# Converting double-precision weights in the first block: a narrower store for the low bits, clamps on GpSimd, casts on ScalarE

## The chip, the cores and the metric

The kernel runs on one core of one Trainium2 chip. The metric is the device time of one execution in microseconds (us); the kernel before takes 967.43 us (median of 3 runs, 966.49 to 967.93). Engines are named as in the profile: PE (TensorE matmuls), PEld (TensorE weight loads), DVE (VectorE), ACT (ScalarE), POOL (GpSimd) and SP (SyncE, which issues the transfers).

## The reference

Windowed attention over 2304 tokens (4 batches of 576, 8 heads of 64, window 64), then two feed-forward networks. The weight matrices arrive as float64, so each number is two 32-bit words; everything else is float32.

```python
h = x @ w_in                                   # 512 -> 2048
g = np.where(h > 0, h, np.exp(np.minimum(h, 0)) - 1)
x = g @ w_out                                  # 2048 -> 512
xn = x / np.sqrt(np.mean(x * x, -1) + 1e-6) * rms_g
gate, val = xn @ w_gate, xn @ w_val            # 512 -> 1536 each
out = (gate / (1 + np.exp(-gate)) * val) @ w_out2
```

## The kernel before

Tokens run through the first network in six blocks of 384. While PE works on a block, the attention of the next block is interleaved with it. A matmul here takes its operands as float32r pairs (a rounded high part and the remainder), three products for each: `mm_in` (line 381) is 12 matmuls of 384 columns for one of the 16 slices f of the hidden layer, `mm_y` (line 408) another 12. Block 1 runs from about 43 to 143 us.

In block 1 the weights of the first network are made as they are needed: the `Feeder` fw1 turns 32 tiles (w_in and w_out for f = 0 to 15) of 128x512 doubles into float32r pairs, which stay for blocks 2 to 6. A second `Feeder`, fwp, does the same for 36 tiles of the second network during blocks 2 to 5 and the start of the last stage; its tiles go on to a scratch tensor `pspill` or `ospill`. One tile takes these steps:

- a transfer brings the raw words (`big`, three buffers, or `tmp`); `lo` is the low word and `hi` the high word of each double
- `s1`: ACT takes the magnitude of `hi` (line 311) and scales the top bits of `lo` to a small integer of 0 to 7, stored as a 32-bit integer over `lo` (line 312); the magnitude is clamped (line 314), on DVE, in fw1 for every second tile on POOL; DVE shifts it left by 3 and ors in the low bits, reading two tensors (line 316)
- `sign` (line 323): DVE ors in the sign bit of `hi`; the raw tile is free after it
- `s2` (line 331): a cast to the high part of the pair, on DVE or ACT as the scheduler chooses
- `s3` (line 337): POOL subtracts to get the remainder

`step` does s3 of tile n-2, s2 of tile n-1 and s1 of tile n, so POOL's queue alternates subtractions and clamps. The tile `wm`, which holds a weight through these steps, has three buffers.

`x_split` (lines 364 and 365) makes the pair of a block's input, 4 casts and 4 subtractions on DVE. `elu` takes a matmul result through ACT (lines 399, 400) and DVE (line 401), and `split_g` makes its pair with a cast (line 390) and a subtraction (line 391) on DVE. A scheduler that simulates the program orders the instructions of every engine from this text; each engine then runs its queue in order. L202 to L224 are the softmax of the attention.

Of the kernel before, what the change touches and what calls it, by code (L numbers as in the profile page):

```python
# [9 lines left out]
F32R = mybir.dt.float32r  # L10
I32 = mybir.dt.int32
U32 = mybir.dt.uint32
AF = mybir.ActivationFunctionType
ALU = mybir.AluOpType
AX = mybir.AxisListType
# [5 lines left out]
def kernel(  # L21
# [17 lines left out]
    nc = tc.nc  # L39
# [9 lines left out]
    scale = 1.0 / float(D) ** 0.5  # L49
    BLOCKS1 = [384]*6  # L50
    MAX_M = (2.0 - 2.0 ** -20) * 2.0 ** 15 / 2.0 ** 112
# [232 lines left out]
    class Feeder:  # L284

        def __init__(self, src, raw, alloc, ahead, pool=False):
            self.pool = pool  # L290
            self.src, self.raw, self.alloc, self.ahead = src, raw, alloc, ahead
            self.n = self.loaded = 0
            self.r, self.m, self.u = {}, {}, {}

        def load(self, upto):
            while self.loaded < min(upto, len(self.src)):
                i = self.loaded
                r = self.raw()
                src = self.src[i][1]
                r = r.bitcast(I32)  # L300
                dst = r
                if len(src.shape) == 3:
                    dst = r.rearrange("p (k f) -> p k f", k=src.shape[1])
                nc.sync.dma_start(out=dst, in_=src)
                self.r[i] = r.rearrange("p (f t) -> p f t", t=2)
                self.loaded += 1

        def s1(self, i):
            lo, hi = self.r[i][:, :, 0], self.r[i][:, :, 1]
            m = mp.tile([128, 512], F32, tag="wm", name="wm", bufs=3)  # L310
            nc.scalar.activation(out=m, in_=hi.bitcast(F32), func=AF.Abs, scale=2.0 ** -112)
            nc.scalar.activation(out=lo, in_=lo.bitcast(U32), func=AF.Copy, scale=0.875 * 2.0 ** -29,
                bias=0.4999)
            (nc.gpsimd if self.pool and i % 2 else nc.vector).tensor_scalar(
                out=m, in0=m, scalar1=MAX_M, scalar2=None, op0=ALU.min)
            nc.vector.scalar_tensor_tensor(
                out=m.bitcast(I32), in0=m.bitcast(I32), scalar=3, in1=lo,
                op0=ALU.logical_shift_left, op1=ALU.bitwise_or)
            self.m[i] = m

        def sign(self, i):
            m, hi = self.m[i], self.r.pop(i)[:, :, 1]
            nc.vector.scalar_tensor_tensor(
                out=m.bitcast(I32), in0=hi, scalar=-2 ** 31, in1=m.bitcast(I32),
                op0=ALU.bitwise_and, op1=ALU.bitwise_or)
            return m

# [29 lines left out]
                self.step()  # L357


    def x_split(xt, n):  # L360
        r = []
        for kk in range(KD):
            xk = mp.tile([128, 2, NMAX], F32R, tag=f"x{kk}", name=f"x{kk}")
            nc.vector.tensor_copy(out=xk[:, 0, :n], in_=xt[:, kk, :n])
            nc.vector.tensor_tensor(
                out=xk[:, 1, :n], in0=xt[:, kk, :n], in1=xk[:, 0, :n].bitcast(F32),
                op=ALU.subtract)
            r.append(xk)
        return r
# [15 lines left out]
    def x_tile():  # L385
        return mp.tile([128, KD, NMAX], F32, tag="xt", name="xt")

    def split_g(src, n, copy):
        g = mp.tile([128, 2, NMAX], F32R, tag="g", name="g", bufs=1 + LAG)
        copy(out=g[:, 0, :n], in_=src[:, :n])  # L390
        nc.vector.tensor_tensor(  # L391
            out=g[:, 1, :n], in0=src[:, :n], in1=g[:, 0, :n].bitcast(F32), op=ALU.subtract)
        return g


    def elu(ph, n):

        e = mp.tile([128, NMAX], F32, tag="e", name="e", bufs=2)
        nc.scalar.activation(out=e[:, :n], in_=ph[:, :n], func=AF.Relu, scale=-1.0)  # L399
        nc.scalar.activation(out=e[:, :n], in_=e[:, :n], func=AF.Exp, scale=-1.0)  # L400
        nc.vector.scalar_tensor_tensor(  # L401
            out=e[:, :n], in0=e[:, :n], scalar=-1.0, in1=ph[:, :n], op0=ALU.add, op1=ALU.max)
        return split_g(e, n, nc.vector.tensor_copy)

    def mm_y(py, wt, g, n, first, last):
        for i, (a, c) in enumerate(((0, 0), (1, 0), (0, 1))):
# [347 lines left out]
    xt = x_tile()  # L754
# [7 lines left out]
        load_v(t)  # L762
    for s in range(NSTART):
        fw1.step()
    xs = x_split(xt, BLOCKS1[0])

    tok0 = 0
    pend = []
# [1 line left out]
    for b, n in enumerate(BLOCKS1):  # L770
        last = b == nblk - 1
        slots = {}
        if not last:
            nn = BLOCKS1[b + 1]
            xt = x_tile()
# [20 lines left out]
        gs = {}  # L796
# [5 lines left out]
        for f in range(F1):  # L802
            fw1.until(("in", f))
            ph = psum("w", 4)
            mm_in(ph, wu[("in", f)], xs, n, f == F1 - 1)
            gs[f] = elu(ph, n)
            run_slot(2 * f)
            if f == F1 - 1 and not last:
                xs_next = x_split(xt, nn)
            if b == 0:  # L810
                fw1.step()
            if f >= LAG:
                fw1.until(("out", f - LAG))
                mm_y(py, wu[("out", f - LAG)], gs.pop(f - LAG), n, f == LAG, False)
            run_slot(2 * f + 1)
            if b == 0:
                fw1.step()
# [7 lines left out]
        if not last:  # L825
            xs = xs_next
# [88 lines left out]
```

## Time and profile before

| what | value |
|---|---|
| median of 3 runs | 967.43 us (966.49 to 967.93) |
| the profiled execution | 967.15 us, its span 965.4 us |
| PE busy, share of the span | 918.5 us, 95% |
| DVE, ACT, POOL busy | 650.4, 491.9, 211.8 us |
| granted TensorE clock, mean | 0.986 of full speed |

The span is the time from the first to the last instruction in the trace; the execution is 1.75 us longer. Matmul ends are modelled, and consecutive matmuls overlap, so PE's busy share overstates how fast it advances: at full clock, 12 matmuls of 384 columns follow one another in 2.08 us. Idle time of an engine that is not the bottleneck costs nothing.

### The profile page before, as it was taken

How to read it: one execution, taken by the hardware profiler on the slowest of the kernel's cores; microseconds unless marked ns; L12 is line 12 of the kernel's file. 1: busy time of each engine (PE TensorE's matmuls, PEld its weight loads, DVE VectorE, ACT ScalarE, POOL GpSimd, SP SyncE). 2: the span in 40 equal slices, each digit the busy share in tenths (PEclk: the TensorE clock that was granted, in tenths of full speed). 3: DMA queues.
4: the chain of work that ended last, by engine and by line, in shares of the span. 5: the costliest groups of instructions: out<-in, count | busy, mean ns of one | idle time of the engine just before them, and what ended most of it. 6: DMA issues, size and time to landing. Idle time of an engine off the chain costs nothing.

```text
span 965.4 us, 16449 instructions
## 1 busy us (share of the span) xinstructions
PE 918.5 (95%) x5916; PEld 863.7 (89%) x5916; DVE 650.4 (67%) x1451; ACT 491.9 (51%) x1199; POOL 211.8 (22%) x228
## 2 busy tenths in 40 slices
PE   6678889999999999999999999999999999999998
PEld 5577789988889998899999999899998998998996
DVE  3899997858867786787788488178363276561461
ACT  5887755665666656566545456344141442341440
POOL 2465760146236114404402100200000000000000
PEclk9789989999999999999999999999999999999999
DMA  9556531765474265536438719781984737945621
GB/s 234 165 167 199 133 108 23 221 194 159 146 228 145 78 197 172 156 103 199 159 122 286 262 48 385 283 349 48 404 328 143 278 124 243 371 141 208 240 70 66
DMA packets 150402, 183.02 MB, mean 190 GB/s; under 512 B 81712, under 2 KB 111408, under 8 KB 150320
## 3 DMA queue, kind: packets, MB, share of 16 engines
q1 hardware_dynamic: 150320, 181.96, 57.3%
q8 instruction: 47, 0.77, 0.3%
q14 instruction: 35, 0.29, 0.1%
HBM read 144.18 MB, written 37.75 MB: 188 GB/s over the span
## 4 chain that ended last, share of the span: by engine, by line
PE 67%; DMA 6%; POOL 4%; ACT 4%; DVE 4%; issue 1%; SPq 0%; POOLq 0%; DVEq 0%; ACTq 0%
PE y L669 16%; PE w L669 12%; PE y L408 11%; PE w L381 10%; PE y L703 10%; PE w L703 5%; DMA pspill<-stg 5%; POOL stg L540 2%; ACT s L206 1%; ACT stg L539 1%; PE w L164 1%; POOL sw L569 1%; PE w L235 1%; PE w L222 1%; PE w L187 1%
## 5 line engine op out<-in xcount | busy, mean ns | idle before, releaser
L381 PE MATMUL w<-x,wu 128*128 128x384 f32 x1152 | 226.8, 345 | 15.3 <-DVE e L401 5.7
L408 PE MATMUL y<-g,wu 128*128 128x384 f32 x1152 | 223.7, 340 | 5.6 <-DVE g L390 3.0
L381 PEld LDWEIGHTS w<-x,wu 128*128 128x128 f32 x1152 | 203.8, 192 | 21.4 <-DVE e L401 6.1
L408 PEld LDWEIGHTS y<-g,wu 128*128 128x128 f32 x1152 | 198.6, 188 | 10.1 <-DVE g L390 4.2
L669 PE MATMUL y<-xw,pu 128*128 128x384 f32 x864 | 161.6, 334 | 0.0
L669 PEld LDWEIGHTS y<-xw,pu 128*128 128x128 f32 x864 | 151.2, 188 | 0.8
L540 POOL TENSOR_TENSOR stg<-wm,stg 128x256 fp32r<-128x256 f32 x72 | 62.5, 873 | 299.9 <-ACT stg L539 299.9
L669 PE MATMUL w<-xw,pu 128*128 128x384 f32 x648 | 123.7, 334 | 0.0
L635 DVE TENSOR_TENSOR c<-c,w 128x384 f32<-128x384 f32 x72 | 39.6, 550 | 118.1 <-PE w L669 117.3
L669 PEld LDWEIGHTS w<-xw,pu 128*128 128x128 f32 x648 | 113.3, 188 | 0.3
L703 PE MATMUL y<-wu,g 128*128 128x512 f32 x432 | 106.4, 390 | 0.0
L703 PEld LDWEIGHTS y<-wu,g 128*128 128x128 f32 x432 | 80.9, 188 | 16.2
L401 DVE SCALAR_TENSOR_TENSOR e<-e,w 128x384 f32<-128x384 f32 x96 | 52.6, 549 | 51.3 <-ACT e L400 50.1
L631 ACT COPY c<-y 128x384 f32<-128x384 f32 x72 | 34.5, 482 | 67.9 <-PE y L669 67.3
L391 DVE TENSOR_TENSOR g<-e,g 128x384 fp32r<-128x384 f32 x96 | 66.0, 689 | 1.8
L399 ACT ACTIVATE e<-w 128x384 f32<-128x384 f32 x96 | 46.3, 484 | 37.2 <-PE w L381 37.1
L337 POOL TENSOR_TENSOR wu<-wm,wu 128x512 fp32r<-128x512 f32 x32 | 47.3, 1489 | 42.7 <-ACT wu L331 27.6
L703 PE MATMUL w<-wu,g 128*128 128x512 f32 x216 | 55.9, 390 | 0.0
L651 ACT CAST g<-e 128x384 fp32r<-128x384 f32 x69 | 34.7, 511 | 37.5 <-DVE e L645 37.5
L206 ACT ACTIVATE s<-s,st 128x128 f32<-128x128 f32 x120 | 46.7, 392 | 10.9 <-DVE st L202 10.9
L640 ACT ACTIVATE e<-c 128x384 f32<-128x384 f32 x54 | 27.5, 524 | 47.1 <-DVE c L635 47.1
L400 ACT ACTIVATE e<-e 128x384 f32<-128x384 f32 x96 | 50.4, 526 | 1.7
(127 smaller groups left out, 1209.1 us busy)
## 6 DMA issues: line engine op xcount, KB each, us to landing
pu<-pspill SPq DMA_DIRECT2D x126, 512.0 KB, 6.5
pspill<-stg SPq DMA_DIRECT2D x84, 256.0 KB, 2.1
wu<-ospill SPq DMA_DIRECT2D x36, 512.0 KB, 5.2
big<-in_moe_w_out_dram SPq DMA_DIRECT2D x16, 512.0 KB, 5.3
big<-in_moe_w_in_dram SPq DMA_DIRECT2D x15, 512.0 KB, 3.8
vw<-in_v_dram SPq DMA_DIRECT2D x27, 256.0 KB, 3.6
tmp<-in_moe_w_out_dram SPq DMA_DIRECT2D x12, 512.0 KB, 4.7
big<-in_moe_w_gate_dram SPq DMA_DIRECT2D x12, 512.0 KB, 5.4
```

The lines of the kernel that those rows point to most:

```text
L206: nc.scalar.activation(out=s[:, p, :], in_=s[:, p, :], func=AF.Exp, scale=-1.0, bias=st[:, 0, p, :], accum_out=st[:, 1, p, :])
L337: eng.tensor_tensor(out=u[:, 1, :], in0=m, in1=u[:, 0, :].bitcast(F32), op=ALU.subtract)
L381: nc.tensor.matmul(pt[:, :n], lhsT=wt[:, a, kk * 128:(kk + 1) * 128], rhs=xs[kk][:, c, :n], start=(i == 0), stop=(i == len(seq) - 1))
L391: nc.vector.tensor_tensor(out=g[:, 1, :n], in0=src[:, :n], in1=g[:, 0, :n].bitcast(F32), op=ALU.subtract)
L399: nc.scalar.activation(out=e[:, :n], in_=ph[:, :n], func=AF.Relu, scale=-1.0)
L400: nc.scalar.activation(out=e[:, :n], in_=e[:, :n], func=AF.Exp, scale=-1.0)
L401: nc.vector.scalar_tensor_tensor(out=e[:, :n], in0=e[:, :n], scalar=-1.0, in1=ph[:, :n], op0=ALU.add, op1=ALU.max)
L408: nc.tensor.matmul(py[m][:, :n], lhsT=wt[:, a, m * 128:(m + 1) * 128], rhs=g[:, c, :n], start=(first and i == 0), stop=(last and i == 2))
L540: nc.gpsimd.tensor_tensor(out=t[:, 1, :], in0=src, in1=t[:, 0, :].bitcast(F32), op=ALU.subtract)
L635: nc.vector.tensor_tensor(out=t, in0=t, in1=bank[b, qi][:, :NB], op=ALU.add)
L669: nc.tensor.matmul(bank[key][:, :NB], lhsT=u[:, qi, a, kk * 128:(kk + 1) * 128], rhs=X[j][kk][:, x, :], start=(first and n == 0), stop=(n ...
L703: nc.tensor.matmul(po[m], lhsT=g[:, a, (m % 3) * 128:(m % 3 + 1) * 128], rhs=w[:, x, :], start=(first and i == 0), stop=(last and i == 2))
```

## The change

The low bits are no longer written over the low word: ACT's second operation stores them as 16-bit integers into the low half of the high word, whose low bits are not needed any more. So the shift on DVE reads one tensor, and `sign` masks the sign and the three low bits in one go (the mask grows by 7). The clamp gets a second operation, a maximum with 0.0, and in fw1 all 32 clamps go to POOL (fwp's stay on DVE). The casts of g in block 1 (16) and of x for blocks 1 and 2 (8) go from DVE to ACT.

```diff
                 self.r[i] = r.rearrange("p (f t) -> p f t", t=2)
+                self.low[i] = r.bitcast(U16).rearrange("p (f t) -> p f t", t=4)[:, :, 2]
...
-            nc.scalar.activation(out=lo, in_=lo.bitcast(U32), func=AF.Copy, scale=0.875 * 2.0 ** -29,
+            nc.scalar.activation(
+                out=self.low[i], in_=lo.bitcast(U32), func=AF.Copy, scale=0.875 * 2.0 ** -29,
                 bias=0.4999)
-            (nc.gpsimd if self.pool and i % 2 else nc.vector).tensor_scalar(
-                out=m, in0=m, scalar1=MAX_M, scalar2=None, op0=ALU.min)
-            nc.vector.scalar_tensor_tensor(
-                out=m.bitcast(I32), in0=m.bitcast(I32), scalar=3, in1=lo,
-                op0=ALU.logical_shift_left, op1=ALU.bitwise_or)
+            (nc.gpsimd if self.pool else nc.vector).tensor_scalar(
+                out=m, in0=m, scalar1=MAX_M, scalar2=0.0, op0=ALU.min, op1=ALU.max)
+            nc.vector.tensor_scalar(
+                out=m.bitcast(I32), in0=m.bitcast(I32), scalar1=3, scalar2=None,
+                op0=ALU.logical_shift_left)
...
-                out=m.bitcast(I32), in0=hi, scalar=-2 ** 31, in1=m.bitcast(I32),
+                out=m.bitcast(I32), in0=hi, scalar=-2 ** 31 + 7, in1=m.bitcast(I32),
...
-    def x_split(xt, n):
+    def x_split(xt, n, copy=nc.vector.tensor_copy):
...
-            nc.vector.tensor_copy(out=xk[:, 0, :n], in_=xt[:, kk, :n])
+            copy(out=xk[:, 0, :n], in_=xt[:, kk, :n])
...
-    def elu(ph, n):
+    def elu(ph, n, copy):
...
-        return split_g(e, n, nc.vector.tensor_copy)
+        return split_g(e, n, copy)
...
-    xs = x_split(xt, BLOCKS1[0])
+    xs = x_split(xt, BLOCKS1[0], nc.scalar.copy)
...
-            gs[f] = elu(ph, n)
+            gs[f] = elu(ph, n, nc.vector.tensor_copy if b else nc.scalar.copy)
...
-                xs_next = x_split(xt, nn)
+                xs_next = x_split(xt, nn, nc.vector.tensor_copy if b else nc.scalar.copy)
```

The scheduler moves instructions with it. POOL at the start of the weights, one clamp (L314 before, L318 now) or subtraction (L337, L342) per row; `wm` and `wu` carry the tile's number. Before:

```order
L314 TENSOR_SCALAR wm_445<-wm_445 128x512
L337 TENSOR_TENSOR wu_443<-wm_437,wu_443 128x512
L337 TENSOR_TENSOR wu_523<-wm_456,wu_523 128x512
L337 TENSOR_TENSOR wu_454<-wm_445,wu_454 128x512
L314 TENSOR_SCALAR wm_525<-wm_525 128x512
L314 TENSOR_SCALAR wm_595<-wm_595 128x512
```

and with the change:

```order
L318 TENSOR_SCALAR wm_437<-wm_437 128x512
L318 TENSOR_SCALAR wm_445<-wm_445 128x512
L318 TENSOR_SCALAR wm_456<-wm_456 128x512
L342 TENSOR_TENSOR wu_443<-wm_437,wu_443 128x512
L342 TENSOR_TENSOR wu_523<-wm_456,wu_523 128x512
L342 TENSOR_TENSOR wu_454<-wm_445,wu_454 128x512
L318 TENSOR_SCALAR wm_525<-wm_525 128x512
L318 TENSOR_SCALAR wm_536<-wm_536 128x512
L318 TENSOR_SCALAR wm_595<-wm_595 128x512
```

Every tile now has its clamp in POOL's queue, three of them ahead of the first subtraction, where one stood.

DVE where block 1 begins (x is the block's input pair, `big` and `tmp` are raw weights). Before:

```order
L314 TENSOR_SCALAR wm<-wm 128x512
L316 SCALAR_TENSOR_TENSOR wm<-wm,tmp_450 128x512
L323 SCALAR_TENSOR_TENSOR wm<-tmp_450,wm 128x512
L316 SCALAR_TENSOR_TENSOR wm<-wm,big_157 128x512
L323 SCALAR_TENSOR_TENSOR wm<-big_157,wm 128x512
L316 SCALAR_TENSOR_TENSOR wm<-wm,big_461 128x512
L364 CAST x_463<-xt 128x384
L364 CAST x_466<-xt 128x384
L364 CAST x_469<-xt 128x384
L364 CAST x_472<-xt 128x384
L323 SCALAR_TENSOR_TENSOR wm<-big_461,wm 128x512
L365 TENSOR_TENSOR x_463<-xt,x_463 128x384
```

and with the change:

```order
L320 TENSOR_SCALAR wm<-wm 128x512
L328 SCALAR_TENSOR_TENSOR wm<-big_157,wm 128x512
L320 TENSOR_SCALAR wm<-wm 128x512
L328 SCALAR_TENSOR_TENSOR wm<-tmp_450,wm 128x512
L370 TENSOR_TENSOR x_463<-xt,x_463 128x384
L370 TENSOR_TENSOR x_466<-xt,x_466 128x384
L320 TENSOR_SCALAR wm<-wm 128x512
L370 TENSOR_TENSOR x_469<-xt,x_469 128x384
```

The clamp and the casts of x are gone from DVE, and the shift (L320) reads `wm` alone. Between the start of block 1 and its end, DVE's queue has 10 casts of weights (L331, now L336) where it had 4; ACT has 6 fewer.

ACT at the first two hidden slices of block 1, with the change (`e` and `g` are a slice's activation and its pair):

```order
L404 ACTIVATE e<-w 128x384 x2
L315 ACTIVATE tmp_600<-tmp_600 128x512
L405 ACTIVATE e<-e 128x384 x2
L395 CAST g<-e 128x384
L314 ACTIVATE wm<-big_611 128x512
L336 CAST wu<-wm 128x512
```

The cast of g (L395) now stands in ACT's queue, between the activations and the next weight.

## Rows read from the trace of the kernel before

**Rows 1.** The page, its first line.

```profile
span 965.4 us, 16449 instructions
```

**Rows 2.** Busy PE, PEld, DVE, ACT, POOL by stretch; granted clock, DMA share, GB/s.

```profile
43.00:143.00 100.00, 85.06 (x600) 78.62 (x600) 97.05 (x188) 72.39 (x170) 64.09 (x42) 0.91 0.53 158
143.00:222.00 79.00, 76.80 (x603) 73.43 (x604) 59.75 (x156) 48.67 (x133) 21.39 (x26) 1.00 0.47 141
222.00:555.00 333.00, 324.44 (x2337) 311.13 (x2336) 254.90 (x605) 193.76 (x505) 103.35 (x122) 1.00 0.55 173
```

**Rows 3.** The waits of PE in 43 to 143 (total us, times, longest).

```profile
PE w L381 <- DVE e L401: 5.7, 2, 4.5
```

**Rows 4.** Groups of DVE in 43 to 143 by form: count | busy, mean | idle.

```profile
L323 DVE SCALAR_TENSOR_TENSOR wm<-big,wm 128x512 int32<-128x512 int32 x17 | 13.9, 824 | 0.1
L316 DVE SCALAR_TENSOR_TENSOR wm<-wm,big 128x512 int32<-128x512 int32 x16 | 13.3, 832 | 0.4 <-POOL wm L314 0.4
L390 DVE CAST g<-e 128x384 fp32r<-128x384 f32 x15 | 11.7, 779 | 0.4
L391 DVE TENSOR_TENSOR g<-e,g 128x384 fp32r<-128x384 f32 x14 | 10.8, 774 | 0.1
L314 DVE TENSOR_SCALAR wm<-wm 128x512 f32<-128x512 f32 x13 | 9.0, 690 | 0.0
L316 DVE SCALAR_TENSOR_TENSOR wm<-wm,tmp 128x512 int32<-128x512 int32 x10 | 8.9, 890 | 0.1
L323 DVE SCALAR_TENSOR_TENSOR wm<-tmp,wm 128x512 int32<-128x512 int32 x10 | 7.7, 772 | 0.0
L331 DVE CAST wu<-wm 128x512 fp32r<-128x512 f32 x4 | 3.2, 788 | 0.0
L364 DVE CAST x<-xt 128x384 fp32r<-128x384 f32 x3 | 3.1, 1072 | 0.0
```

**Rows 5.** POOL operations in 43 to 143, duration min/median/max in ns.

```profile
L314 POOL TENSOR_SCALAR wm<-wm x13: 1490/1782/2044, 48.4 to 136.7; 128x512 f32<-128x512 f32 x13
L337 POOL TENSOR_TENSOR wu<-wm,wu x29: 1277/1470/1860, 42.6 to 143.0; 128x512 fp32r<-128x512 f32 x29
```

**Rows 6.** DVE operations over the whole span, duration min/median/max in ns.

```profile
L316 DVE SCALAR_TENSOR_TENSOR wm<-wm,big x55: 675/686/1775, 22.1 to 606.2; 128x512 int32<-128x512 int32 x55
L323 DVE SCALAR_TENSOR_TENSOR wm<-big,wm x55: 652/691/1761, 22.8 to 606.9; 128x512 int32<-128x512 int32 x55
L390 DVE CAST g<-e x96: 344/360/1454, 57.3 to 548.5; 128x384 fp32r<-128x384 f32 x96
L391 DVE TENSOR_TENSOR g<-e,g x96: 542/558/1654, 60.0 to 548.9; 128x384 fp32r<-128x384 f32 x96
L314 DVE TENSOR_SCALAR wm<-wm x52: 395/426/1514, 15.9 to 605.7; 128x512 f32<-128x512 f32 x52
```

**Rows 7.** DVE beside POOL in order of time, 65 to 70 (start, duration).

```profile
65.33 3.38 POOL L337 TENSOR_TENSOR wu<-wm,wu 128x512 fp32r<-128x512 f32 x2
...
67.47 1.45 DVE L390 CAST g<-e 128x384 fp32r<-128x384 f32 x1
```

**Rows 8.** ACT: two groups of 43 to 143, and the page's g cast.

```profile
L331 ACT CAST wu<-wm 128x512 fp32r<-128x512 f32 x24 | 14.8, 617 | 14.7 <-DVE wm L323 14.7
L312 ACT ACTIVATE big<-big 128x512 int32<-128x512 uint32 x15 | 10.3, 684 | 5.9 <-DMA big<-in_moe_w_out_dram 3.0 <-DMA big<-in_moe_w_in_dram 2.8
...
L651 ACT CAST g<-e 128x384 fp32r<-128x384 f32 x69 | 34.7, 511 | 37.5 <-DVE e L645 37.5
```

**Rows 9.** DVE in order of time, 22.0 to 24.6, ahead of a softmax.

```profile
22.08 0.69 DVE L316 SCALAR_TENSOR_TENSOR wm<-wm,big 128x512 int32<-128x512 int32 x1 [1.38 <-ACT tmp L312]
24.54 0.28 DVE L202 CUSTOM_DVE_ANT_0 tmp<-w,mask 128x128 f32<-128x128 f32 x1
```

**Rows 10.** The chain that ended last in 43 to 143 (start, us).

```profile
125.00 3.59 DMA big<-in_moe_w_in_dram
```

**Rows 11.** A POOL operation on 256 columns, min/median/max in ns.

```profile
L569 POOL TENSOR_TENSOR sw<-sw,wm x12: 727/738/868, 191.1 to 462.5; 128x256 f32<-128x256 f32 x12
```

More of the change, by code (lines that the diff above doesn't have):

```diff
@@ L12 @@
 U32 = mybir.dt.uint32
+U16 = mybir.dt.uint16
 AF = mybir.ActivationFunctionType
@@ L292, in __init__ @@
             self.n = self.loaded = 0
-            self.r, self.m, self.u = {}, {}, {}
+            self.r, self.low, self.m, self.u = {}, {}, {}, {}
         def load(self, upto):
```

## The prediction

> **What bounds the kernel now.** I read the page first, then the table of busy time by stretch, then, for the one stretch that stands out, the waits of PE and the groups of DVE, POOL and ACT. The profiled execution takes 967.15 us, 0.28 below the median of the runs; its span is 965.4 [rows 1], and the sums below are made against it. By stretch [rows 2], PE is idle for 2.2 us of 79 in block 2 and for 8.6 of 333 in blocks 3 to 6, always at the full clock: PE sets the time there. Block 1, from 43 to 143 us, is different: PE is idle for 15 of 100 us and granted 0.91 of its clock, while DVE is busy for 97.05. PE's longest wait is for DVE (the activation at L401, 5.7 us) [rows 3]. So block 1 runs at DVE's pace. Block 2, which does the same matmuls and as much attention, takes some 80 us: about 20 us is the most that block 1 can give, and what it gives goes one for one to the end, since PE sets the pace of what follows.
>
> DVE is slow there partly because it waits inside its instructions. The cast of g takes 0.344 us at best but 0.779 on average in block 1 [rows 4, 6]; one that started during POOL's subtractions took 1.45 [rows 7]. Its wait is counted as busy time. Against the shortest duration of each [rows 6], the 26 shifts (13.3 + 8.9 us), 27 signs (13.9 + 7.7), 15 casts of g, 14 subtractions of g and 13 clamps of block 1 [rows 4] carry 4.7 + 4.0 + 6.5 + 3.2 + 3.9 = 22.3 us of waiting, beside 42 POOL operations: 0.53 us for each.
>
> **The change, part by part, in block 1.** DVE, from 97.05 us:
> - 13 clamps leave: -9.0 [rows 4].
> - 15 casts of g leave: -11.7; 3 casts of x (the fourth ran just before 43): -3.1 [rows 4].
> - 26 shifts read one tensor in place of two. No row shows a one-tensor shift. The nearest is the clamp, one input and one output of the same size, 0.690 on average [rows 4]: 26 x 0.690 = 17.9 in place of 22.2, so -4.3. The ends: nothing if it runs as it does now, and -11.9 if each reaches the clamp's best 0.395 [rows 6]. I take -4.3, because the same neighbour on POOL stays.
> - 6 casts of weights come from ACT by the scheduler's choice: 6 x 0.788 = +4.7 [rows 4].
> - 15 more POOL operations in the stretch (28 clamps in place of 13, the first 4 lying ahead of it): 15 x 0.53 = +8.0 of waiting.
>
> That leaves DVE at 81.7, say 82 us.
>
> POOL, now 64 us [rows 2], does 29 subtractions and 28 clamps. At the shortest durations [rows 5] that is 29 x 1.277 + 28 x 1.490 = 78.8 us, at the medians 29 x 1.470 + 28 x 1.782 = 92.5. Waiting for DVE makes the difference, and DVE gets some 15 us lighter, so I take the middle, 86. This prices the clamp with its second operation like the clamp with one. No row shows the dearer form; the ends are 0.727, the shortest POOL operation on half the columns [rows 11], and 2 x 1.490 = 2.98, a whole second pass. I take the one-operation price since it is the same tile on the same engine.
>
> ACT, 72.4 us [rows 2]: 15 casts of g and 3 of x at 0.511, less 6 casts of weights at 0.617 [rows 8]: +9.2 - 3.7 = 78 us. Its store of the low bits is priced as before, 0.684 [rows 8]: the same count of elements, every 8 bytes. If the narrow store took half as long again, 26 x 0.34 = 9 us would bring ACT to 87, level with POOL; if it were half as long, nothing would follow, since ACT would not be the bound.
>
> The longest queue becomes POOL with 86 us. DVE, which sets the pace now, is busy for 97% of the stretch; at that share block 1 takes 86 / 0.97 = 89 us, 11 less. Raw buffers work the same way: on the chain that ended last, a transfer of 3.59 us [rows 10] waits for a sign to free its buffer, and a clamp that takes 1.5 us on POOL in place of 0.4 on DVE lengthens that loop for half the tiles. I leave this inside the 3%.
>
> Ahead of block 1, DVE spends 22.08 to 24.54 on weights before it starts the softmax that ACT waits for [rows 9]. Of these four operations the clamp goes, a shift gets cheaper and one moves behind: 1 us, with 0 and 1.4 as ends.
>
> After block 1, 36 shifts of the second network's tiles get 0.26 us cheaper (medians 0.686 and 0.426 [rows 6]), and 4 casts of x for block 2 move. PE covers all this [rows 2]: 0. If PE's idle 10.8 us of blocks 2 to 6 shifted with the reordered queues, I allow 2 either way.
>
> **Sum:** 967.15 - 11 - 1 = 955.2; with the 0.28 us to the median, **955.5 us**. Without a row for the price of the new clamp, 950 to 961 is this case's own range (POOL from 81 to 91 us).
>
> The Trainium skill (SBUF — State Buffer, Who interferes with whom) speaks against the change: a GpSimd operation and a VectorE operation that reads two tensors from SBUF, or runs with two ports, exclude each other, and the later one fully blocks until the first is done. The trace agrees for single operations (1.45 us against 0.344), but on average 0.53 us of waiting falls to each POOL operation; if the rule held for each in full, the sum would be that of the third rival.
>
> **The rivals.**
>
> 1. *POOL has time to spare* (faster). Were the clamp with two operations as short as the lower end, 0.727, POOL would need 28 x 0.727 + 37.0 to 42.6 = 57 to 63 us and bind nothing; DVE with 82 would, and block 1 takes 82 / 0.97 = 84.5: 967.15 - 15.5 - 1 + 0.28 = 951. For it: the clamp with one input is slower on POOL than the subtraction with two, 1.490 against 1.277 [rows 5], so its time is not set by how much it reads. Against it: no row has it shorter. The Trainium skill (GPSIMD Engine Reference, section 3.1, Elementwise) says that up to two operations per element GpSimd is bound by its port, and gives 769 ns for 512 elements; by that price POOL's clamps would sum to 21.5 us and the time would be 951 too. The one-operation row here, 1.490 us, does not agree with it.
>
> 2. *The second operation costs a second pass on POOL* (slower). At 2.98 us a clamp POOL would need 28 x 2.98 + 37.0 = 120.4 us, block 1 124, and the kernel 967.4 + 24 - 1 = 990. It decides from the point where POOL's sum passes the 97 us that DVE has now: (97 - 42.6) / 28 = 1.94 us for a clamp at the median subtraction, 2.14 at the shortest. Between them and 2.98, say 2.3 us, it is 28 x 2.3 + 29 x 1.38 = 104, block 1 108, the kernel 974. For it: 1.94 is only 0.16 above the clamp's present median. Against it: the engine's queue is idle for 36 of 100 us now, and DVE gets lighter.
>
> 3. *The lock hands the gain back* (no change). If each of the 15 added POOL operations stops DVE for its whole 1.49 us and not for 0.53, DVE gets 22.4 in place of 8.0 and stands at 96, block 1 at 99: 967.4 - 1 - 1 = 965.5 to 967. For it: the single row of 1.45 us. Against it: the average over 42 operations.
>
> 4. *The change does not reach the end.* If block 1 shortens but its rest waits for transfers of raw weights, the gain is cut; the transfers fill 0.53 of their engines there [rows 2], which leaves room. I count this in the third.
>
> **How the numbers follow.** The forecast gets 0.38, the first rival 0.28, the third (with the fourth) 0.16, the second 0.18. A measurement of this kernel can tell 0.2%, some 2 us, from no change. Faster by over 0.2%: 0.38 + 0.28 + 0.06 of the third = 0.72; within it 0.10; slower 0.18. The range reaches from 946 (the first rival with a shift at its lower end and 2 us from the later blocks) to 968 (the third); only the second rival and a little at the lower end, some 0.2, lie outside.
>
> **What would show it.** The POOL clamp's duration decides first: 1.5 to 1.8 us is the forecast, 0.8 or less the first rival, over 1.9 the second. DVE busy in block 1 should fall to about 82 us in a stretch of some 89, POOL rise to 86, ACT to 78, PE's granted clock rise above 0.91, the casts of g on DVE be gone until block 2, and block 2 keep its length. DVE at 95 or more would speak for the third. The prediction is wrong if block 1 keeps its 100 us, or if blocks 2 to 6 change by over 3 us.

## The result, and the profile after

The changed kernel takes 975.65 us (median of 4 runs, 973.38 to 975.96) beside 967.68 us of the kernel before on the same chip (4 runs, 966.49 to 968.50): a ratio of 1.0078, 95% interval 1.0060 to 1.0097. It is 8 us slower. The forecast was 955.5 us, the range 946 to 968. The profiled execution took 975.55 us, its span is 973.8 us.

Line numbers after: abs L314, store of the low bits L315, clamp L318, shift L320, `sign` L328, cast L336, subtraction L342, casts of x L369, of g L395, `e` L404 to L406, `mm_in` L386, `mm_y` L413.

The same stretches as [rows 2], first PE, PEld, DVE, ACT, POOL, then granted clock, DMA share and GB/s:

```profile
43.00:143.00 100.00, 85.18 (x598) 77.70 (x597) 76.85 (x160) 91.82 (x182) 55.22 (x53) 0.93 0.51 148
143.00:222.00 79.00, 75.28 (x593) 71.54 (x592) 57.68 (x152) 52.20 (x133) 21.62 (x26) 1.00 0.47 141
222.00:555.00 333.00, 319.93 (x2298) 306.75 (x2297) 247.74 (x595) 208.00 (x503) 103.89 (x123) 0.99 0.53 166
```

DVE fell from 97 to 77 us, POOL from 64 to 55, and ACT rose from 72 to 92. PE did not get further in its 100 us. Its waits in 43 to 143 name another engine than [rows 3]:

```profile
PE y L413 <- ACT wu L336: 4.9, 4, 2.3
PE w L386 <- ACT wu L336: 4.3, 4, 1.6
```

The groups of ACT in the same stretch, as [rows 8], show why:

```profile
L315 ACT ACTIVATE big<-big 128x512 uint16<-128x512 uint32 x16 | 22.1, 1384 | 0.2
L315 ACT ACTIVATE tmp<-tmp 128x512 uint16<-128x512 uint32 x10 | 13.9, 1388 | 0.0
L336 ACT CAST wu<-wm 128x512 fp32r<-128x512 f32 x18 | 11.3, 626 | 1.7 <-DVE wm L328 1.6
L395 ACT CAST g<-e 128x384 fp32r<-128x384 f32 x15 | 8.2, 543 | 1.7 <-DVE e L406 1.6
```

The store as 16-bit numbers takes 1.38 us, where the store as 32-bit numbers took 0.684 [rows 8]; 26 of them are 36 us of ACT's 92. The casts of g and of weights cost about what they did before. DVE (groups as [rows 4]) and POOL (minimum, median, maximum in ns, as [rows 5]):

```profile
L320 DVE TENSOR_SCALAR wm<-wm 128x512 int32<-128x512 int32 x25 | 19.3, 774 | 4.5 <-POOL wm L318 4.5
L328 DVE SCALAR_TENSOR_TENSOR wm<-big,wm 128x512 int32<-128x512 int32 x16 | 14.3, 891 | 0.3
L406 DVE SCALAR_TENSOR_TENSOR e<-e,w 128x384 f32<-128x384 f32 x15 | 8.3, 552 | 13.5 <-ACT e L405 13.5
```

```profile
L318 POOL TENSOR_SCALAR wm<-wm x26: 604/628/1085, 44.4 to 137.5; 128x512 f32<-128x512 f32 x26
L342 POOL TENSOR_TENSOR wu<-wm,wu x27: 1271/1298/1734, 43.1 to 142.5; 128x512 fp32r<-128x512 f32 x27
```

The clamp with two operations takes 0.63 us on POOL; with one it took 1.78 [rows 5]. DVE now stands idle for 13.5 us until ACT has an activation ready.

**Where the 8 us lie.** 192 executions of each of the `mm_in` and `mm_y` lines make a block. Counted off in the traces, the last `mm_y` of each block is reached at these times (us from the span's start):

| block | 1 | 2 | 3 | 4 | 5 | 6 |
|---|---|---|---|---|---|---|
| before | 151.6 | 234.3 | 320.4 | 404.3 | 485.7 | 552.6 |
| after | 152.2 | 236.5 | 323.9 | 408.5 | 493.9 | 560.8 |

Block 1 ends 0.6 us later, blocks 2 to 5 together take 341.7 us in place of 334.1, and block 6 is unchanged. So two things want explaining: why block 1 gains nothing from 20 us less on DVE, and why blocks 2 to 5, whose loss I had forecast as zero, take 7.6 us more.

Blocks 2 to 5 before and after, in the columns of the first table:

```profile
151.60:485.70 334.10, 323.66 (x2491) 307.47 (x2490) 254.49 (x638) 206.37 (x560) 112.27 (x136) 1.00 0.52 159
```

```profile
152.20:493.90 341.70, 324.91 (x2484) 308.76 (x2483) 250.03 (x637) 221.29 (x558) 114.22 (x136) 0.99 0.51 155
```

ACT is busy for 14.9 us more; 26 stores at 0.70 us more each are 18. It is idle for a third of the time even so. But PE's idle time grew from 10.4 to 16.8 us. One such place in ACT's queue (start, duration, in brackets the idle time ahead):

```profile
282.49 0.41 ACT L544 CAST stg<-sw 128x256 fp32r<-128x256 f32 x1 [1.68 <-POOL sw L574]
282.80 0.58 ACT L225 COPY pT<-w 128x512 f32<-128x512 f32 x1
285.51 0.40 ACT L544 CAST stg<-wm 128x256 fp32r<-128x256 f32 x1 [2.13 <-DMA pspill<-stg]
285.82 0.48 ACT L404 ACTIVATE e<-w 128x384 f32<-128x384 f32 x1
286.20 0.58 ACT L172 COPY kT<-w 128x512 f32<-128x512 f32 x1
286.67 0.53 ACT L405 ACTIVATE e<-e 128x384 f32<-128x384 f32 x1
287.09 0.58 ACT L174 COPY qT<-w 128x512 f32<-128x512 f32 x1
```

and PE beside it:

```profile
284.13 1.15 PE L236 MATMUL w<-pT,vw 128*64 128x64 f32 x32
287.73 3.12 PE L386 MATMUL w<-x,wu 128*128 128x384 f32 x12 [2.45 <-ACT qT L174]
```

A cast into a staging buffer of the second network (`stg`, two buffers) stands 2.13 us until the transfer to the scratch tensor frees its buffer. Behind it in the same queue are the activation of h and the two copies out of PSUM that PE needs. PE stops for 2.45 us, and its next 12 matmuls then take 3.12 us, where a row of twelve elsewhere shows 2.24:

```profile
319.89 2.24 PE L386 MATMUL w<-x,wu 128*128 128x384 f32 x12
```

The granted clock of 288.2 to 296.2 is 0.79, so a part of it ran at the lower of the two levels (1.2 and 2.4 GHz), after 1.00 in the 8 us before. Here one wait is paid twice. That isn't the rule: two pauses of 2.34 and 2.44 us in the same blocks were followed by 8 us at a granted clock of 1.00, and at this place the kernel before has a pause too, of 1.46 us. The three waits for the copies in the attention (`kT` before, `qT` after) grew by 3.0 us, not by the whole loss:

```profile
PE w L381 <- ACT kT L177: 4.2, 3, 1.6
```

```profile
PE w L386 <- ACT qT L174: 7.2, 3, 2.4
```

Another 3.8 us lie in shorter waits of PE for DVE (2.0 us before, 5.8 after); how the stores lengthen those was not traced.

### The profile page after: what moved, and what is told of

Read it like the earlier page. It is cut to its first block, busy times and chain, and to the rows that moved or that the text cites. A ratio compares the mean times of both kernels' runs of the same rounds, so it can differ in the third digit from the quotient of the medians.

```text
span 973.8 us, 16471 instructions
## 1 busy us (share of the span) xinstructions
PE 922.7 (95%) x5916; PEld 866.4 (89%) x5916; DVE 621.4 (64%) x1418; ACT 538.1 (55%) x1216; POOL 203.5 (21%) x244
## 4 chain that ended last, share of the span: by engine, by line
PE 67%; ACT 15%; DMA 7%; POOL 4%; issue 3%; DVE 3%; SPq 0%; POOLq 0%; ACTq 0%; DVEq 0%
PE y L674 15%; PE w L674 12%; PE w L386 11%; PE y L413 10%; PE y L708 10%; PE w L708 5%; DMA pspill<-stg 4%; ACT wm L314 3%; POOL stg L545 2%; ACT big L315 2%; ACT tmp L315 2%; ACT s L207 2%; ACT e L404 1%; ACT e L405 1%; DMA big<-in_moe_w_gate_dram 1%
## 5 line engine op out<-in xcount | busy, mean ns | idle before, releaser
L386 PE MATMUL w<-x,wu 128*128 128x384 f32 x1152 | 228.3, 346 | 19.2 <-ACT qT L174 7.2
L413 PE MATMUL y<-g,wu 128*128 128x384 f32 x1152 | 225.6, 342 | 10.2 <-ACT wu L336 4.9
L386 PEld LDWEIGHTS w<-x,wu 128*128 128x128 f32 x1152 | 204.2, 192 | 25.6 <-ACT qT L174 7.6
L413 PEld LDWEIGHTS y<-g,wu 128*128 128x128 f32 x1152 | 199.5, 189 | 16.6 <-ACT wu L336 5.9
L406 DVE SCALAR_TENSOR_TENSOR e<-e,w 128x384 f32<-128x384 f32 x96 | 52.9, 551 | 75.1 <-ACT e L405 74.0
L315 ACT ACTIVATE big<-big 128x512 uint16<-128x512 uint32 x55 | 75.9, 1381 | 0.7
L404 ACT ACTIVATE e<-w 128x384 f32<-128x384 f32 x96 | 47.5, 496 | 40.9 <-PE w L386 36.5
L544 ACT CAST stg<-wm 128x256 fp32r<-128x256 f32 x72 | 29.1, 409 | 46.2 <-DMA pspill<-stg 31.9
L342 POOL TENSOR_TENSOR wu<-wm,wu 128x512 fp32r<-128x512 f32 x32 | 44.3, 1387 | 46.0 <-ACT wu L336 27.6
```

The lines of the kernel that those rows point to most:

```text
L315: nc.scalar.activation(out=self.low[i], in_=lo.bitcast(U32), func=AF.Copy, scale=0.875 * 2.0 ** -29, bias=0.4999)
L342: eng.tensor_tensor(out=u[:, 1, :], in0=m, in1=u[:, 0, :].bitcast(F32), op=ALU.subtract)
L386: nc.tensor.matmul(pt[:, :n], lhsT=wt[:, a, kk * 128:(kk + 1) * 128], rhs=xs[kk][:, c, :n], start=(i == 0), stop=(i == len(seq) - 1))
L406: nc.vector.scalar_tensor_tensor(out=e[:, :n], in0=e[:, :n], scalar=-1.0, in1=ph[:, :n], op0=ALU.add, op1=ALU.max)
L413: nc.tensor.matmul(py[m][:, :n], lhsT=wt[:, a, m * 128:(m + 1) * 128], rhs=g[:, c, :n], start=(first and i == 0), stop=(last and i == 2))
```

## The experiments

The theories that the expectations name: **A**, the 16-bit store fills ACT, and ACT sets block 1's pace; **A2**, the loss sits in blocks 2 to 5, through the second network's stores; **B**, the casts on ACT are too much; **C**, the clamps on POOL hold DVE up; **D**, the three `wm` buffers set block 1's pace; **E**, it is the order of the queues and the hops between engines. A *miss* is a measurement outside the range that a theory had named. Times in the text are medians; block times come from the one profiled execution of each, and since single runs of one kernel often lie 2 to 3 us from its median, smaller differences of a block are not read.

### Each part alone, and the change without one

**e1_wide**: the change with the 32-bit store, the shift that reads two tensors and the old mask (not in the cut below), so that POOL's clamps and ACT's casts are what remains.

```diff
-                out=self.low[i], in_=lo.bitcast(U32), func=AF.Copy, scale=0.875 * 2.0 ** -29,
+                out=lo, in_=lo.bitcast(U32), func=AF.Copy, scale=0.875 * 2.0 ** -29,
...
-            nc.vector.tensor_scalar(
-                out=m.bitcast(I32), in0=m.bitcast(I32), scalar1=3, scalar2=None,
-                op0=ALU.logical_shift_left)
+            nc.vector.scalar_tensor_tensor(
+                out=m.bitcast(I32), in0=m.bitcast(I32), scalar=3, in1=lo,
+                op0=ALU.logical_shift_left, op1=ALU.bitwise_or)
```

> The low bits are stored again as 32-bit integers over the low word and the shift reads two tensors; clamps with two operations on POOL and casts on ACT stay. Theory A (the 16-bit store, 1.38 us in place of 0.68, makes ACT the queue that sets block 1 and delays the later blocks): ACT in block 1 falls from 92 to some 76 us, block 1 from 100 to 85 or 90 us, blocks 2 to 6 return to their old length, 952 to 960 us in all. Theory B (the casts moved to ACT are what is too much for it): 970 us or more. Theory C (32 clamps on POOL hold DVE's ports and give back what they save): no better than 966.

Measured: 974.28 us (970.75 to 977.94, 6 runs), ratio 1.0076 (1.0055 to 1.0096). Block 1 ends at 158.8, 7.2 us later than before; blocks 2 to 5 take 334.0 us, as before. Its block 1:

```profile
43.00:143.00 100.00, 83.54 (x557) 74.57 (x556) 77.80 (x147) 75.50 (x177) 55.60 (x50) 0.90 0.51 150
```

No engine but PE is busy for over 78% of it, and still block 1 is longer than before. For block 1 theory A misses: with ACT relieved, something holds it that is no engine's sum. For blocks 2 to 5 it is right. B and C had this time in their ranges; the next runs take the two parts one by one.

**e2_narrow_only**: before with the 16-bit store, the one-tensor shift and the wider mask; clamps and casts as before.

> The kernel before with the 16-bit store alone (and with it the one-tensor shift and the wider sign mask). Theory A: the store takes 1.38 us in all 68 tiles; block 1 stays near 100 us because DVE and ACT are both near 92, and blocks 3 to 5 get longer by 4 to 8 us in sum, 970 to 978 us. Theory B: ACT without the casts has room, 965 to 968. Theory C says nothing of it.

Measured: 977.73 us (975.60 to 979.30, 5 runs), ratio 1.0107 (1.0090 to 1.0124). Block 1 ends at 149.9, and blocks 2 to 5 take 346.1 us, 12 more than before. This part alone costs all that the change costs, and costs it outside block 1, as A had it (blocks 3 to 5 take 7.9 us more, of its 4 to 8).

**e3_clamps_only**: before with the two-operation clamps, all of the first network's on POOL.

> The kernel before with the clamps alone: two operations, all 32 of the first network on POOL. Theory A: the clamp takes 0.63 us on POOL in place of 1.49, DVE loses 9 us of clamps and much of its waiting; block 1 falls to 85 to 92 us, 954 to 961 us in all. Theory C: DVE's waiting grows by what the clamps saved, 966 or more. Theory B says nothing of it.

Measured: 969.75 us (967.25 to 974.77, 12 runs), ratio 1.0018 (1.0005 to 1.0032). The profiled execution is the slowest of the twelve, so its block 1 (157.0) says little. DVE is busy for 85 of 100 us and POOL for 59; nothing is gained, so A misses and the time is in C's range. C's mechanism is there in part: in this execution the shifts and signs of block 1 sum to 25.9 and 24.9 us, 7 us more than before [rows 4], against the 9.0 us of clamps that left. But DVE's sum fell all the same.

**e4_casts_only**: before with the casts of g and x on ACT, as in the change.

> The kernel before with the casts alone: g in block 1 and x for blocks 1 and 2 on ACT. Theory A: DVE loses 15 us in block 1, ACT rises from 72 to about 80, block 1 falls to 88 to 93 us, 956 to 962 us in all. Theory B: ACT holds up the activations, 969 us or more.

Measured: 968.00 us (965.84 to 969.27, 12 runs), ratio 1.0006 (0.9996 to 1.0015). Block 1 ends at 151.3. Both ranges miss, and B falls: by themselves the casts cost nothing, and give nothing.

**e5_narrow_fw1**: the change, but with the 16-bit store and the one-tensor shift in the first network only; the second network's 36 tiles as before.

```diff
+            if self.pool:
                 nc.scalar.activation(
                     out=self.low[i], in_=lo.bitcast(U32), func=AF.Copy, scale=0.875 * 2.0 ** -29,
                     bias=0.4999)
+            else:
+                nc.scalar.activation(out=lo, in_=lo.bitcast(U32), func=AF.Copy, scale=0.875 * 2.0 ** -29,
+                    bias=0.4999)
```

> The changed kernel with the 16-bit store and the one-tensor shift in the first network's tiles alone; the second network's 36 tiles get the 32-bit store and the shift that reads two tensors. Theory A2 (the 8 us are lost in blocks 2 to 5, where ACT's store is 0.7 us longer in each of the second network's tiles and PE waits for ACT's copies behind it): block 1 as in the changed kernel, blocks 2 to 5 as before, 966 to 969 us. Rival: the loss comes from block 1's reordered start into block 2, then 973 us or more remain.

Measured: 967.72 us (965.13 to 969.66, 12 runs), ratio 1.0000 (0.9989 to 1.0011). Block 1 ends at 151.6 and blocks 2 to 5 take 334.6 us. A2 holds: the 16-bit store in the second network's tiles costs the whole 8 us, and block 1 of the change is worth nothing either way.

### The prices by themselves

**p1_prices**: before, with the operations in question run three times each behind the last output, on data that is there.

> The kernel before, and behind its last output, when the engines are idle, three times each: ACT's store of the low bits as 32-bit at 8 bytes, 16-bit at 8 bytes, 16-bit at 4 bytes, 16-bit packed, 32-bit packed and bfloat16 at 8 bytes; POOL's clamp with one and with two operations; DVE's one-tensor shift. If the 16-bit store is dear because it writes half of a word, the packed one takes 0.68 us and the one at 4 bytes 1.38; if it is the integer type, packed takes 1.38 too and bfloat16 0.68. POOL's clamp: 1.49 us with one operation, 0.60 with two. The shift: 0.42 us.

ACT first, 512 numbers of 32 bits read at every 8 bytes (minimum, median, maximum in ns): L896 writes 32-bit numbers every 8 bytes, L899 16-bit every 8, L902 16-bit every 4, L905 16-bit side by side, L907 32-bit side by side, L909 bf16 every 8. Then POOL's clamp with one operation (L913) and with two (L916).

```profile
L896 ACT ACTIVATE probe<-slot x3: 673/704/719, 963.0 to 972.1; 128x512 int32<-128x512 uint32 x3
L899 ACT ACTIVATE probe<-slot x3: 1313/1317/1336, 963.6 to 972.7; 128x512 uint16<-128x512 uint32 x3
L902 ACT ACTIVATE probe<-slot x3: 820/826/827, 964.7 to 973.7; 128x512 uint16<-128x512 uint32 x3
L905 ACT ACTIVATE probe<-slot x3: 628/631/632, 965.4 to 974.4; 128x512 uint16<-128x512 uint32 x3
L907 ACT ACTIVATE probe<-slot x3: 643/648/648, 965.9 to 974.9; 128x512 int32<-128x512 uint32 x3
L909 ACT ACTIVATE probe<-slot x3: 1320/1325/1327, 966.5 to 975.5; 128x512 bf16<-128x512 uint32 x3
L913 POOL TENSOR_SCALAR probe<-slot x3: 1480/1485/1651, 961.7 to 966.1; 128x512 f32<-128x512 f32 x3
L916 POOL TENSOR_SCALAR probe<-slot x3: 608/609/777, 963.2 to 967.6; 128x512 f32<-128x512 f32 x3
```

Neither the type nor the stride is dear alone: 16-bit numbers side by side take 0.63 us, 32-bit numbers every 8 bytes 0.70. Two bytes written at every eighth take 1.32. And the clamp with one operation takes more than twice as long as the one with two, here with hardly a neighbour (three shifts on DVE ran in the same 6 us). Of the expectations, two missed: at every 4 bytes the store takes 0.83 and not 1.38, and the shift, beside POOL's clamps, took 0.57 and twice 0.82 us and not 0.42. The run takes 979.42 us, the probes included.

The Trainium skill (ScalarE: Activation LUTs, section What ACT_TABLE_LOAD costs) gives one element per cycle for every function, with constant scale and bias 186 ns and 0.833 ns for each column: 613 ns for 512, an estimate from that page. The rows for outputs side by side (0.63 and 0.65) agree; the strided 16-bit output is not covered by it.

### Block 1 and the buffers of `wm`

A tile takes a `wm` buffer at abs and gives it back after the subtraction. Averaged over tiles 7 to 31 of the first network, from the start of abs to the end of the subtraction, and from there to the abs that takes the buffer next (operations paired in the order in which they ran):

| kernel | buffers | held, us | free, us | (held + free) / buffers | a tile every | block 1 ends |
|---|---|---|---|---|---|---|
| before | 3 | 9.79 | 1.37 | 3.72 | 3.70 | 151.6 |
| after | 3 | 9.40 | 1.86 | 3.75 | 3.78 | 152.2 |
| e1_wide | 3 | 10.03 | 2.18 | 4.07 | 4.04 | 158.8 |
| s8_wide_2wm | 2 | 7.52 | 1.09 | 4.31 | 4.34 | 168.7 |
| s7_wide_4wm_1stg | 4 | 11.13 | 3.84 | 3.75 | 3.85 | 151.0 |
| s1_wide_5wm | 5 | 12.35 | 5.67 | 3.60 | 3.66 | 147.6 |

The two rates agree because a buffer goes round as tiles go through, so their agreement proves nothing. With two or three buffers one is taken again 1 to 2 us after it came free, and with four and five it lies there for 4 to 6. The lower three rows are the experiments that follow.

**e7_wide_buf** and **e8_before_buf**: `wm` of the first 20 tiles from the pool of the finished weights, so that no tile waits for one of three buffers; on e1_wide and on before.

```diff
-            m = mp.tile([128, 512], F32, tag="wm", name="wm", bufs=3)
+            if self.pool and i < 20:
+                m = wp.tile([128, 1024], F32, tag="wu", name="wm")[:, 0:512]
+            else:
+                m = mp.tile([128, 512], F32, tag="wm", name="wm", bufs=3)
```

> 32-bit store, clamps on POOL, casts on ACT (the first experiment of this list) and for the first 20 tiles a weight buffer of its own in place of one of three. Theory D (block 1 goes at the pace of three weight buffers: a tile holds one for about 10 us and 2 more pass until it is taken again, so one tile per 4 us, whatever engine is free): the first 20 tiles run at 2.5 to 3 us each, block 1 loses 10 to 20 us, 953 to 964 us. Rival E (queue order and hops between engines set the pace, not the buffers): 971 us or more.

> The kernel before with the same extra weight buffers. Theory D: DVE is busy for 97 of 100 us, so buffers give little here, 0 to 4 us: 963 to 968 us. If buffers alone set the pace in every version it gains as much as the wide version does, 955 us or less. Rival E: no change, 966 to 969 us.

Measured: 1007.10 us (1005.85 to 1007.96, 4 runs) and 998.26 us (997.94 to 1001.32, 4 runs). D misses in both, and E in the second. The scheduler laid these tiles out almost one after the other: the first abs comes at 32 us and not at 15, a tile follows every 4.5 and 4.1 us, and block 1 ended at 193.0 and 180.3. So they are no test of D. But with more buffers than e1_wide and before, block 1 ends 34 and 29 us later, so the order of the queues can do much by itself, which is E's point.

**s1_wide_5wm**: e1_wide with five buffers, which `wm` and the staging tiles share (the same memory as three and two).

```diff
-            m = mp.tile([128, 512], F32, tag="wm", name="wm", bufs=3)
+            m = mp.tile([128, 512], F32, tag="wm", name="wm", bufs=5)
...
-        t = mp.tile([128, 2, 256], F32R, tag="stg", name="stg", bufs=2)
+        t = mp.tile([128, 2, 256], F32R, tag="wm", name="stg", bufs=5)
```

> 32-bit store, clamps on POOL, casts on ACT, and the weight tile's three buffers and the two of the staging tile (which is idle in block 1) made one set of five. Theory D (in block 1 a tile holds one of three buffers for 10 us, so one tile passes per 3.4 to 4 us although no engine is full): with five, block 1 falls from 110 us to 85 to 92, then DVE or PE sets it; 948 to 960 us. Rival E (the order of the queues and the hops between engines set the pace): block 1 stays over 105 us, 968 us or more.

Measured: 963.92 us (961.60 to 965.20, 6 runs), ratio 0.9954 (0.9938 to 0.9971): faster than both kernels. Block 1 ends 11.2 us earlier than in e1_wide (D had 18 to 25), blocks 2 to 5 take 332.6 us. The time lies between the ranges of D and E, and the profiled execution is the fastest of the six. The same stretch:

```profile
43.00:143.00 100.00, 88.09 (x630) 83.68 (x627) 90.06 (x162) 82.18 (x194) 59.68 (x52) 0.93 0.52 153
```

All engines do more in the same 100 us, and DVE is once more the fullest.

**s7_wide_4wm_1stg**: e1_wide with four `wm` buffers and one for staging, not shared. **s8_wide_2wm**: e1_wide with two `wm` buffers.

> The change with the 32-bit store and the two-tensor shift, as in e1_wide, but four wm buffers and one stg buffer, each with its own tag: nothing is shared in block 1. Theory D (the three wm buffers set the pace of block 1 once no engine is full): block 1 ends at 147 to 152 us in place of e1_wide's 158.8, as with the five shared buffers (147.6). Rival (s1_wide_5wm gained through the sharing of wm and stg, or through another order): block 1 ends within 2 us of 158.8. With one stg buffer blocks 2 to 5 should get longer, since every staging cast then waits for the transfer of the one before it: total 968 to 985 by D, 980 or more by the rival.

> e1_wide with two wm buffers in place of three, the opposite test. In e1_wide a tile holds its buffer for 10.03 us and the next one takes it 2.18 us later, three buffers, so 4.04 us per tile. Theory D: with two buffers it is (10.0 + 2.2) / 2 = 6.1 us per tile if the steps take as long, at least 5.0 if the shorter queues cut the buffer's cycle to 10 us; 32 tiles then make block 1 longer by 30 to 65 us and the time 1000 to 1040 us. Rival (queue order and not buffers): within 10 us of e1_wide's 974.

Measured: s7 995.58 us (989.36 to 996.68, 4 runs), s8 996.24 us (one run). Block 1 of s7 ends at 151.0, as D had it; its total is above what D expected, because with one staging buffer blocks 2 to 5 take 339.6 us, block 6 takes 77.0 in place of 66.8, and all that follows 426.7 in place of 412.8, a larger loss than I had priced. In s8 block 1 ends at 168.7: 10 us later than in e1_wide, where D had 30 to 65, since a tile comes every 4.34 us and not every 5 or more (a buffer is held for 7.52 us and not 10); blocks 2 to 5, which use `wm` too, take 346.1. The 996.24 us are just below D's 1000 and well above the rival's range. PE's longest waits in block 1 of s8 are for the steps of the weights:

```profile
PE w L385 <- ACT wu L335: 12.1, 9, 2.7
PE w L385 <- POOL wu L341: 5.1, 7, 1.4
```

With 2, 3, 4 and 5 buffers and no other edit that touches block 1, it ends at 168.7, 158.8, 151.0 and 147.6. So the number of buffers moves block 1. It doesn't do so in e1_wide by making an engine wait for one, as D has it. Abs on ACT takes the buffer, and a subtraction on POOL frees it. From 15 to 165 us ACT stands idle ahead of abs in e1_wide for a transfer alone, and in s8 for that subtraction, 4.7 us in 5 places (1.5 us before, 0.3 in the change):

```profile
L314 ACT ACTIVATE wm<-big x19: 647/663/721, 19.2 to 146.2; 128x512 f32<-128x512 f32 x19
L314 ACT ACTIVATE wm<-tmp x13: 644/665/722, 15.4 to 117.3; 128x512 f32<-128x512 f32 x13
  DMA big<-in_moe_w_in_dram: 1.8, 1
```

```profile
  POOL wu L341: 4.7, 5
```

No abs of e1_wide starts less than 0.3 us after its buffer came free. What is left is that the scheduler, which simulates the program with these buffers, orders the queues by them, and the engines then run that order: closer to E than to D. No run kept the order and altered the buffers, so this is not shown, and why e1_wide's order is 7 us worse than that of before or of the change stays open. Transfers of raw weights, the prediction's fourth rival, made ACT wait in block 1 for 9.5 us before and 2.6 in the change: they are not what keeps the change from gaining.

### Five shared buffers in the other versions

**s6_after_5wm** is the change itself, **s4_fw1_5wm** e5_narrow_fw1, **s2_before_5wm** before, **s3_clamps_5wm** e3_clamps_only and **s5_casts_5wm** e4_casts_only, each with the edit of s1_wide_5wm.

> The changed kernel whole, with five buffers. Theory A2: blocks 2 to 5 keep most of the 8 us that the 16-bit store costs there; 966 to 975 us, and 6 to 9 us above the version with the narrow store in the first network alone. Rival: more staging buffers free ACT from its waits there, and the two versions are within 3 us.

> The change with the 16-bit store in the first network's tiles alone, and five buffers. Theory A for block 1 (ACT, 92 of 100 us busy with stores of 1.38 us, sets its pace): block 1 loses 3 to 7 us at most, 960 to 966 us. If ACT's load is not what sets it and buffers are, it falls as far as the wide version, 950 to 958 us.

> The kernel before with the same set of five buffers. Theory D with DVE as the bound beside it: DVE is busy for 97 of 100 us, so block 1 loses at most 4 us, 962 to 967 us. If the buffers alone set the pace before the change too: 950 to 958 us.

> Before with the two-operation clamps, all on POOL in the first network (as e3_clamps_only), and five buffers for wm and stg together. Theory D with DVE as the next limit: e3_clamps_only had DVE busy for 85 of 100 us and block 1 to 157.0 us; with five buffers block 1 ends at 147 to 151 and the time is 962 to 966 us, so that the casts on ACT are not needed for the gain. Rival (DVE must be lightened by the casts too, as s2_before_5wm, which starts block 1 4 us late and ends it at 164): 970 to 980 us.

> Before with the casts of g and x of the first block on ACT (as e4_casts_only) and five buffers for wm and stg together. If DVE sets the pace (92 of 100 us in e4_casts_only), five buffers change block 1 by under 2 us from 151.3, or start it some 4 us later as in s2_before_5wm: 966 to 972 us. If the buffers set it (a tile's cycle of 7.92 + 2.88 us over three buffers gave 3.76 us per tile), block 1 ends at 144 to 149 and the time is 960 to 966 us.

| run | time, us | ratio to before | block 1 ends | blocks 2 to 5 |
|---|---|---|---|---|
| s6_after_5wm | 968.40 (966.51 to 971.72, 12) | 1.0005 (0.9993 to 1.0017) | 152.3 | 333.3 |
| s4_fw1_5wm | 970.14 (966.72 to 973.57, 12) | 1.0020 (1.0007 to 1.0033) | 153.0 | 335.7 |
| s2_before_5wm | 981.13 (977.00 to 983.18, 6) | 1.0128 (1.0106 to 1.0150) | 164.3 | 335.8 |
| s3_clamps_5wm | 968.98 (966.25 to 972.92, 10) | 1.0011 (0.9993 to 1.0030) | 152.2 | 333.3 |
| s5_casts_5wm | 978.84 (977.85 to 982.03, 4) | 1.0117 (1.0091 to 1.0142) | 157.7 | 338.7 |

s6 is in A2's range of time, but it is not 6 us above s4; the rival (within 3 us) is right. s4, s2 and s5 lie above all that was named for them, and s3 lies between its two ranges. Three things follow.

In **s6** block 1 ends where it ended with three buffers (152.3 and 152.2). From 43 us to there ACT is busy for 98.6 of 109.3 us: with the 16-bit store ACT holds block 1, and more buffers don't help. That is theory A. The pair e1_wide and s1_wide_5wm, without that store, gains 11 us from the same edit; and s1_wide_5wm and s6, which differ by that store and what goes with it (shift and mask), end block 1 at 147.6 and 152.3 and are 4.5 us apart in all.

In **s6** the loss of blocks 2 to 5 is gone too (333.3 us), although every 16-bit store is still there. PE is idle for 10.2 of them, as before the change:

```profile
152.30:485.60 333.30, 323.14 (x2488) 309.41 (x2487) 240.33 (x638) 220.12 (x559) 108.33 (x136) 0.99 0.52 159
```

ACT's wait for a staging buffer falls from 43.4 us in blocks 2 to 5 of the change to 7.2:

```profile
ACT stg L544 <- DMA pspill<-stg: 43.4, 38, 3.6
```

```profile
ACT stg L544 <- DMA pspill<-stg: 7.2, 9, 2.1
```

This is not yet the path of the loss. Before had that wait as well (46.0 us) without the loss; in s6 the same casts wait longer for POOL (29.3 us in place of 13.5); and PE's three waits for `qT`, the kind shown above at 287 us, stay as long as in the change:

```profile
PE w L386 <- ACT qT L174: 7.1, 3, 3.8
```

What is shown is that the 7.6 us need both the 16-bit store in the second network's tiles (e5_narrow_fw1) and the separate three and two buffers (s6). Whether the `wm` or the staging buffers take the loss away, and through which waits, was not tried: the edit gives more of both and reorders the queues.

**s2** and **s5** got slower with five buffers, against what I expected of both. Their weights are done long before they are used: the last subtraction of the first network ends at 140.8 us in s2 and at 136.2 in s5, while block 1 ends at 164.3 and 157.7 (in s1 it is 143.4 and 147.6). The first `mm_y` comes at 67.8 and 73.7 us, before at 60.3. In s2 PE waits for g:

```profile
PE y L408 <- DVE g L390: 10.4, 4, 7.5
```

My reading, not tried by itself, is that with buffers to spare DVE's queue takes up weights ahead of the block's own activations, as it still does every second clamp; s1, s3, s4 and s6, where POOL clamps all, didn't get slower in this way. s3, without the casts on ACT, gains nothing (DVE is busy for 99.9 of the 109.2 us from 43 to the end of block 1), so the gain of s1 takes all three: the clamps on POOL, the casts on ACT, and the buffers. Why the scheduler orders s2 and s5 so was not looked into further.

## Why the prediction was wrong

- **The step that failed first** is ACT's: "its store of the low bits is priced as before, 0.684". It measured 1.38, outside my bound too (half as long again, 1.03). 26 stores at 0.70 more are 18 us; ACT came to 92 in the 100 us (forecast 78), and to 97.5 of the 109.2 us up to the end of block 1. With this one price put right, my own sum would have read (78 + 18) / 0.97 = 99 us for block 1: no gain.
- **The step that made it slower** is "After block 1 ... PE covers all this: 0", with 2 us allowed. I counted the 36 shifts that get cheaper, and not the 36 stores that get dearer on ACT. Blocks 2 to 5 took 7.6 us more: 6.3 of PE's idle time and 1.3 of its busy time. e5_narrow_fw1 (967.72 against 975.65) puts all of the 8 us there; the path from the store to PE is shown only in part (3.0 us of longer waits for `qT`).
- **The form of the sum**, the longest queue divided by 0.97, failed as well, since "block 1 runs at DVE's pace" was half of the truth. DVE fell to 76.85 us, even below my 82, and block 1 ended 0.6 us later. In e1_wide the store has the price that I forecast and no queue but PE's is over 78 us, so the sum gives 80 us, and block 1 ended 7.2 us later than before. The number of `wm` buffers, which my sum doesn't have, moves it by 3 to 10 us a step; through the order of the queues, as far as the traces tell. Even s1_wide_5wm, with the forecast's price for the store and five buffers, gains 4 us and not the 12 of the forecast.
- **POOL's 86 us** were wrong as well: the clamp takes 0.63 and not 1.49 to 1.78, and POOL stands at 55. The first rival had this price (0.727) and so the right mechanism on POOL, and the wrong end, since POOL's spare time was not what was missing. Here the Trainium skill (GPSIMD Engine Reference, section 3.1, Elementwise; 769 ns for 512 elements) was nearer to the measured 0.61 and 0.63 than the price that I took, and doesn't hold for the clamp with one operation (1.485 alone in p1_prices).
- **Right**: DVE's terms (the clamps and casts leave, a shift at 0.774 where 0.690 was taken, 9 casts of weights stand where 4 stood), the casts of g on ACT at 0.543. The third rival did not come about: the waiting inside DVE's shifts, signs and subtractions of g, against the shortest of each, came to 17 us beside 53 POOL operations, 0.32 for each, so my 0.53 was too high as well; POOL's clamps are shorter now. The slower rival that I gave a price, a second pass on POOL, had the wrong engine. None of the rivals was the one that happened: an output that is dearer to write, on an engine that the sum held to have room, and in tiles of later blocks that the sum left out.

## What to carry to other kernels

Look for a row of the very output that an operation will write, its element size and stride, before pricing it by its count of elements, and count a shared helper's edit in every stage that calls it, not only in the one it was meant for. Where work runs in steps over several engines, a change in the number of buffers can move a stage in which no instruction waits for a buffer (here, as far as the traces tell, because the scheduler lays out another order): look in the trace whether anything waited before blaming the buffers. Relieving one limit of a stage need not give anything: here clamps and casts gave nothing each alone, cost 7 us together, and gained 4 us once two more buffers stood beside them.

## What the runs showed of the hardware

- An ACT operation that writes 16-bit numbers at every 8 bytes takes 1.32 us for 128x512, at every 4 bytes 0.83, side by side 0.63; 32-bit numbers at every 8 bytes take 0.70. bf16 behaves like the 16-bit integers (p1_prices).
- On POOL a minimum with one constant takes 1.485 us for 128x512, a minimum and a maximum in one operation 0.609.
- In the change, a pause of PE of 2.45 us was followed by a granted clock of 0.79 over 8 us, with 12 matmuls in 3.12 us in place of 2.24; pauses of 2.34 and 2.44 us in the same run were followed by 8 us at 1.00.
